# Gated SSM-convolution and shift-MLP kernel: the last transform step on two column tiles, its rows put in place by SBUF transfers, W4 in three tiles, and a new order of steps behind step 480

## The chip, the cores and the metric

The kernel runs on one core of a Trainium2 chip. The metric is the device time of one execution in microseconds (us). The engines are TensorE (PE; PEld is its weight load), VectorE (DVE), ScalarE (ACT), GpSimd (POOL) and SyncE (SP), which here issues nearly all DMAs.

## The reference, cut to what matters

```python
# q = B's x = A_q: 1 x 2048 x 640 (bf16); w1, w2: 640x640; w3: 640x1536; w4: 1536x640
def reference(A_q, A_k, A_v, A_shift_k, A_ssm_k, A_ssm_D, B_x, B_w1, B_w2, B_w3, B_w4, gate_w):
    x = A_q
    g = sigmoid((x * gate_w).sum(-1, keepdims=True))
    # a: a 4-tap shift of k, times v, a causal convolution over the 2048 rows, times q
    kv = shift4(A_k, A_shift_k) * A_v
    y = irfft(rfft(pad(kv), axis=1) * rfft(pad(A_ssm_k)).T)[:, :2048] + kv * A_ssm_D
    a = x * y
    # b: MLP with a row shift per quarter of the columns, then a second MLP
    h = gelu(layernorm(x) @ w1)
    x1 = x + shift_rows_by_quarter(h) @ w2
    b = x1 + gelu(layernorm(x1) @ w3) @ w4
    return g * a + (1 - g) * b
```

## The kernel before, in words

The 2048 rows lie as 128 partitions times 16 tiles `t1` (row = 16 p + t1), 640 columns each; four tiles are a chunk `c`. The result is built in place in the tile X (X1 is the same tile).

The convolution is a transform in four matmul steps with scratch in HBM between them. `step1` transforms the convolution's taps and kv along the partitions (scratch S_h, S_x). `gather` reads both back in blocks of 640 KB, `step2` transforms them along the tiles, `product` multiplies the two spectra on DVE, `step3` is the first half of the inverse and sends its blocks to the scratch S_g (8 sends, L523), and `gin` reads S_g back (L537) in three tiles: gin0 for t1 0 to 7, gin1 for t1 8 to 13, gin2 for t1 14 and 15, each by four loads `a` = 0 to 3. Load `a` needs the sends of the step3 calls 2a and 2a+1. gin1 lies in the place of W3, so its loads wait for the last matmul of `w3`.

`step4(t1)` is the last half of the inverse. A tile of 640 columns is done in two halves of 320. For each half the table F4 (128x128 bf16, two versions with zeros in every other column) is used in two matmuls, r = 0 and 1, that add up in one PSUM bank (L893). The row parity r thereby comes out interleaved on the partitions, as the rows of X lie. A half is then evicted in one of two ways: ACT copies it with the gate's factor as scale and DVE multiplies the copy with q (L897, L900), or DVE does both in one instruction on PSUM (L903). One DVE addition of 128x640 puts the tile onto X (L907).

The MLP runs beside it: `w3(c, f)` is five matmuls of 512 columns and a gelu on ACT (L840, L844), `w4(t1)` two halves of twelve matmuls of 320 columns and a DVE update of X (L867, L870; t1 = 14 is split into 512 and 128 columns and comes last). W4 is one tile of 1920 KB in the place of WA, which holds W1, W2 and a mixed part of W1; its one load (L216) therefore waits for the last matmul of `w2`.

The order of everything is a written list ORDER of 1099 names `call.arguments:step`. Each engine and SP executes its instructions in the order of this list and waits in place. SLOTS gives by hand which of 8 PSUM banks ("c") and which ring buffer each new tile takes. PE works in shapes: full 128x128 (`w3`, `w4`, `step4`), row tiles of 64 partitions (`step1`), 64x32 (`step2`) and 32x64 (`step3`).

## Time and profile before

| | before |
|---|---|
| times of three runs | 227.29, 228.85, 229.12 us (median 228.85) |
| profiled execution | 227.13 us, of which the span from first to last instruction is 225.4 us |
| PE, DVE, ACT busy | 217.8, 183.7, 171.4 us |
| PE share of the chain that ended last | 79% |
| bytes moved | 57.61 MB, mean 256 GB/s |
| granted TensorE clock | 1.000 |

A row of the chain of waits or of the timeline starts with its start and its length in us from the span's start. A row of the groups reads: line, engine, operation, out<-in, shapes, count | busy us, mean ns of one | idle us of that engine before it. A DMA row ends with KB of one transfer and the us from issue to landing.

### The profile page before, as it was taken

Reading aid. Unit: us, or ns where it says so; the run is one execution under the profiler, and the core shown is the slowest. Engines: PE = TensorE matmul, PEld = TensorE weight load, DVE = VectorE, ACT = ScalarE, POOL = GpSimd, SP = SyncE. Lnnn points to the kernel's source line nnn. Section 1 sums busy time; section 2 is a strip of 40 time slices with the busy share of each in tenths; the row PEclk is TensorE's granted clock in tenths of the full one; section 3 lists DMA queues with packets and bytes.
Section 4 is the critical chain, followed back from the end, with each engine's and each line's share of the span. In section 5 each row is a group of like instructions: output and inputs, shape, how many; then the busy total and the mean of one; then the engine's idle time right before and its main releaser. Section 6 shows DMA issues by size and latency. Waiting matters only on the chain.

```text
span 225.4 us, 6053 instructions
## 1 busy us (share of the span) xinstructions
PE 217.8 (97%) x2427; PEld 121.5 (54%) x2428; DVE 183.7 (81%) x447; ACT 171.4 (76%) x341; POOL 38.1 (17%) x91
## 2 busy tenths in 40 slices
PE   8989999899999999999999999999999999999994
PEld 2557455447846563345664444556533547657762
DVE  7898998868889969963899988989999841439994
ACT  4899988787999999999987597967988450266450
POOL 4247246816000431300600000000000000000000
PEclk9999999999999999999999999999999999999999
DMA  6999998892998999999989570690794879429914
GB/s 226 374 376 344 258 280 170 317 364 107 361 365 355 348 295 265 410 334 343 254 219 338 116 243 0 191 379 17 119 305 166 249 259 366 175 60 305 324 70 179
DMA packets 41770, 57.61 MB, mean 256 GB/s; under 512 B 18446, under 2 KB 34446, under 8 KB 41486
## 3 DMA queue, kind: packets, MB, share of 16 engines
q1 hardware_dynamic: 41166, 54.60, 75.4%
q0 software_dynamic: 576, 2.62, 3.1%
q8 instruction: 19, 0.31, 0.6%
q14 instruction: 9, 0.07, 0.1%
HBM read 34.93 MB, written 18.35 MB: 236 GB/s over the span
## 4 chain that ended last, share of the span: by engine, by line
PE 79%; DMA 9%; DVE 4%; ACT 4%; issue 1%; POOL 1%; SPq 0%; ACTq 0%
PE ps L840 24%; PE ps L867 23%; PE psw L788 7%; PE ps L465 5%; PE ps L893 4%; DMA X<-in_A_q_dram 4%; PE psm L707 4%; DMA xt<-xn 3%; PE psz L228 3%; PE ps L512 3%; PE ps L423 2%; PE pst L390 2%; DVE X L791 2%; ACT stg L360 2%; DMA S_x<-stg 2%; PE psk L590 1%
## 5 line engine op out<-in xcount | busy, mean ns | idle before, releaser
L840 PE MATMUL ps<-x1t,W 128*128 128x512 bf16 x240 | 56.1, 380 | 0.1
L867 PE MATMUL ps<-W,gt 128*128 128x320 bf16 (+2 forms) x383 | 55.1, 299 | 0.1
L867 PEld LDWEIGHTS <-gt 128*128 128x128 bf16 x384 | 36.2, 98 | 17.7 <-issue 3.0
L844 ACT ACTIVATE gt<-ps 128x512 bf16<-128x512 f32 x48 | 27.6, 609 | 19.0 <-PE ps L867 10.6
L840 PEld LDWEIGHTS <-W 128*128 128x128 bf16 x240 | 21.9, 98 | 28.7 <-issue 5.9
L360 ACT CAST stg<-ps 128x512 bf16<-128x512 f32 x55 | 28.6, 604 | 2.3 <-PE ps L423 2.0
L870 DVE SCALAR_TENSOR_TENSOR X<-ps,OMG,X 128x320 bf16<-128x320 f32 (+2 forms) x32 | 17.2, 547 | 11.9 <-PE ps L867 11.7
L707 PE MATMUL psm<-xt,WA 128*128 128x512 bf16 x100 | 23.4, 379 | 1.9 <-DMA WA<-in_B_w_dram 0.8
L360 ACT CAST gs<-ps 128x320 bf16<-128x320 f32 x41 | 15.6, 440 | 8.8 <-PE ps L512 4.8
L788 PE MATMUL psw<-WA,HT 128*128 128x320 bf16 x116 | 21.4, 300 | 0.0
L362 DVE CAST XS<-ps 128x512 bf16<-128x512 f32 x19 | 12.5, 684 | 6.7 <-PE ps L465 6.7
L362 DVE CAST stg<-ps 128x512 bf16<-128x512 f32 x25 | 15.8, 683 | 1.9 <-PE ps L423 1.9
L707 PEld LDWEIGHTS <-WA 128*128 128x128 bf16 x100 | 9.2, 97 | 12.9 <-DMA WA<-in_B_w_dram 1.0
L360 ACT CAST hs<-ps 128x512 bf16<-128x512 f32 x28 | 15.0, 605 | 1.4 <-PE ps L465 1.4
L791 DVE SCALAR_TENSOR_TENSOR X<-psw,X 128x320 bf16<-128x320 f32 x32 | 14.5, 487 | 1.6 <-PE psw L788 1.6
L897 ACT ACTIVATE y<-ps,GS 128x320 bf16<-128x320 f32 x22 | 10.4, 526 | 5.7 <-PE ps L893 3.5
L710 ACT ACTIVATE HT<-psm 128x512 bf16<-128x512 f32 x20 | 11.8, 617 | 3.6 <-PE psm L707 3.5
L788 PEld LDWEIGHTS <-HT 128*128 128x128 bf16 x116 | 10.7, 98 | 6.8 <-issue 3.1
L362 DVE CAST gs<-ps 128x320 bf16<-128x320 f32 x23 | 10.7, 484 | 2.4 <-PE ps L512 1.7
L797 ACT ACTIVATE jk<-X 128x640 bf16<-128x640 bf16 x16 | 12.2, 761 | 0.5 <-DVE X L791 0.4
L788 PE MATMUL psw<-WA,HM 128*128 128x320 bf16 x44 | 12.3, 299 | 0.0
L360 ACT CAST XS<-ps 128x512 bf16<-128x512 f32 x21 | 11.8, 607 | 0.5 <-PE ps L465 0.3
(151 smaller groups left out, 346.6 us busy)
## 6 DMA issues: line engine op xcount, KB each, us to landing
S_x<-stg SPq DMA_DIRECT2D x8, 640.0 KB, 4.3
S_h<-stg SPq DMA_DIRECT2D x8, 640.0 KB, 4.8
ax<-S_x SPq DMA_DIRECT2D x8, 640.0 KB, 5.9
ax<-S_h SPq DMA_DIRECT2D x8, 640.0 KB, 8.1
S_g<-gs SPq DMA_DIRECT2D x8, 640.0 KB, 3.6
W<-in_B_w_dram SPq DMA_DIRECT2D x2, 1920.0 KB, 9.1
kn<-in_A_k_dram SPq DMA_DIRECT2D x4, 640.0 KB, 6.9
E<-in_A_ssm_k_dram SPq DMA_DIRECT2D x5, 512.0 KB, 6.1
```

Of the source, the lines that this page charges most:

```text
L360: A.copy(out=dst, in_=src)
L362: V.tensor_copy(out=dst, in_=src)
L465: PE.matmul(ps[j][q:q + 32, lo - 512 * u:hi - 512 * u], lhsT=CMP[HALF[j], 8 * b + 4 * h + i, c, :], rhs=st[name, 2 * b + h][HALF[j], i, lo ...
L707: PE.matmul(ps[:].rearrange("p (a b) -> p a b", a=4), lhsT=W1N[:, k, 160 * u:160 * u + P] if u < 4 else W1M[:, k, :], rhs=xt[:, :, k, :], ...
L710: A.activation(out=st["HT"][:, 4 * c:4 * c + 4, u, :], in_=ps[:].rearrange("p (t b) -> p t b", t=4), func=ACT.Gelu_apprx_tanh)
L788: PE.matmul(ps[:], lhsT=h_tile(f, t1), rhs=W2P[:, f, o:o + W], start=(f == 0), stop=(f == 4))
L791: V.scalar_tensor_tensor(out=X1[:, t1, o:o + W], in0=box["ps"][:], scalar=1.0, in1=X[:, t1, o:o + W], op0=ALU.mult, op1=ALU.add, accum_out ...
L797: A.activation(out=jk[:], in_=X1[:, t1, :], func=ACT.Square, accum_out=S12[:, 1, t1:t1 + 1])
L840: PE.matmul(ps[:].rearrange("p (a b) -> p a b", a=4), lhsT=st["W3"][:, k, f * P:(f + 1) * P], rhs=xt[:, :, k, :], start=(k == 0), stop=(k ...
L844: A.activation(out=st["gt", c, f // 4][:, f % 4, :], in_=ps[:], func=ACT.Gelu_apprx_tanh)
L867: PE.matmul(ps[:], lhsT=st["gt", c, f // 4][:, f % 4, i * P:(i + 1) * P], rhs=st["W4"][:, f, o:o + w], start=(f == 0), stop=(f == FC - 1))
L870: V.scalar_tensor_tensor(out=X1[:, t1, o:o + w], in0=box["ps"][:], scalar=OMG[:, t1:t1 + 1], in1=X1[:, t1, o:o + w], op0=ALU.mult, op1=ALU ...
```

## The change

Up to step 480 of ORDER (about 89 us into the span) the two kernels do the same work in the same order. The change has three parts.

1. `step4` now takes a chunk of four tiles. For each half of 320 columns the two parities r are two matmuls of 128x64 weights into the two partition halves of one bank, on two column tiles. The eviction (ACT or DVE) scales by GSP, the gate's factor in the order of parities, into a tile `ys`. When the eight halves of a chunk are evicted, two DMAs of 64 partitions and 320 KB each (L907 of the changed kernel) put the even and the odd rows in place in a tile YP. Then DVE multiplies with q in two instructions of 128x1280 and adds to X in two more.
2. WA is three tiles, and W4 comes in three loads of 800, 800 and 320 KB into them.
3. ORDER has 1074 names, in a new order behind step 480.

```diff
-    F4 = const.tile([P, 2, H, 2], BF16, name="F4")
+    F4 = const.tile([P, H], BF16, name="F4")
+    GSP = const.tile([P, NT], F32, name="GSP")
...
-    WA = main.tile([P, DC * (2 * D + P)], BF16, name="WA", tag="WA")
...
+    WN = main.tile([P, DC, D], BF16, name="WN", tag="WN")
+    WP = main.tile([P, DC, D], BF16, name="WP", tag="WP")
+    WM = main.tile([P, DC, P], BF16, name="WM", tag="WM")
+    W1N, W2P, W1M = WN[:], WP[:], WM[:]
...
-    def load_w4():
-        st["W4"] = main.tile([P, FC, D], BF16, name="W4", tag="WA")
-        SP.dma_start(out=st["W4"][:], in_=B_w4.rearrange("(kt p) e -> p kt e", p=P))
+    def load_w4(u):
+        n, w = ((0, DC), (DC, DC), (2 * DC, 2))[u]
+        st["W4", u] = main.tile([P, w, D], BF16, name="W4" + "abc"[u], tag=("WN", "WP", "WM")[u])
+        SP.dma_start(out=st["W4", u][:], in_=B_w4.rearrange("(kt p) e -> p kt e", p=P)[:, n:n + w, :])
...
-        V.memset(F4[:], 0.0)
-        yield from sin_table(F4[:, 0, :, 0], n, 256)
-        A.activation(out=F4[:, 1, :, 1], in_=n[:], func=ACT.Sin, scale=TWO_PI / 256 * SH, bias=NPI[:])
+        yield from sin_table(F4[:], n, 256)
...
+        yield
+        for r in range(2):
+            SP.dma_start(out=GSP[HALF[r], :], in_=GS[r:P:2, :])
...
-    def step4(t1, ev):
...
-                    PE.matmul(ps[:], lhsT=F4[:, r].rearrange("p a b -> p (a b)"), rhs=g[:, r, o + 320 * v:o + 320 * v + 320], start=(r == 0), stop=(r == 1))
...
+    def step4(c, ev):
+        box = {}
+        def make(u):
+            t1, w = 4 * c + u // 2, slice(320 * (u % 2), 320 * (u % 2) + 320)
+            part = [z for z in range(3) if GIN[z][0] <= t1][-1]
+            o = (t1 - GIN[part][0]) * D + 320 * (u % 2)
+            ps = []
+            def first():
+                ps.append(slot(psc, [P, 320], F32, "ps5", "c", 8))
                 for r in range(2):
+                    PE.matmul(ps[0][HALF[r], :], lhsT=F4[:], rhs=st["gin", part][:, r, o:o + 320], start=True, stop=True, tile_position=(0, H * r))
+            def second():
+                if "ys" not in box:
+                    box["ys"] = slot(pool("L2"), [P, 4, D], BF16, "hs", "hp", 4)
+                scaled(ev[u], box["ys"][:, u // 2, w], ps[0][:], GSP[:, t1:t1 + 1])
+            return [first, second]
+        def send():
+            if "YP" not in st:
+                st["YP"] = main.tile([P, 4, 4, D], BF16, name="YP", tag="RT")
+            for r in range(2):
+                SP.dma_start(out=flat(st["YP"][r:P:2, c]), in_=flat(box["ys"][HALF[r]]))
+        def times(h):
+            y = st["YP"][:, c, 2 * h:2 * h + 2, :]
+            V.tensor_tensor(out=y, in0=y, in1=st["q2", c][:, 2 * h:2 * h + 2, :], op=ALU.mult)
+        def total(h):
+            x = X1[:, 4 * c + 2 * h:4 * c + 2 * h + 2, :]
+            V.tensor_tensor(out=x, in0=x, in1=st["YP"][:, c, 2 * h:2 * h + 2, :], op=ALU.add)
+        return banks(8, make, [send, lambda: times(0), lambda: times(1), lambda: total(0), lambda: total(1)])
...
-        "step1.HT0.0.VAAVVAVAVV:12 "
-        "w3.0.6:1 "
...
+        "step1.HT0.1.VVAAAAAAVA:16 load_w4.1:0 w3.0.8:0 w3.0.8:1 w3.0.6:1 step1.HT0.0.VAAVVVVAAV:7 w2.15:4 w3.0.4:0 "
...
```

The following pieces show the order of instructions at the three places that the prediction speaks of. S_h, S_x and S_g are the scratches, stg and gs what is sent to them, ax and gin what is read back, ys appears under the name hs, q2 is q.

SP's queue around the load of W4, before (from about 90 us into the span):

```order
L437 DMA S_h_69<-stg_1726 128x2560
L437 DMA S_h_69<-stg_1812 128x2560
L437 DMA S_h_69<-stg_1844 128x2560
L216 DMA W4_2090<-in_B_w4_dram 128x12x640
L444 DMA ax_2138<-S_h_69 128x4x640
```

and in the changed kernel:

```order
L218 DMA W4b_1845<-in_B_w4_dram 128x5x640
L437 DMA S_h_69<-stg_1727 128x2560
L218 DMA W4c_1980<-in_B_w4_dram 128x2x640
L437 DMA S_h_69<-stg_1813 128x2560
L437 DMA S_h_69<-stg_1842 128x2560
L218 DMA W4a_2155<-in_B_w4_dram 128x5x640
L444 DMA ax_2189<-S_h_69 128x4x640
```

Two of the three parts of W4 now stand ahead of the last sends to S_h, which the first read of S_h waits for.

SP's queue from the last sends to S_g to the end, before:

```order
L523 DMA S_g_71<-gs_3601 128x4x640
L876 DMA q2_3757<-in_A_q_dram 128x2560
L537 DMA gin0_3437<-S_g_71 32x2x5120 x2
L537 DMA gin2_3568<-S_g_71 32x2x1280
L876 DMA q2_3819<-in_A_q_dram 128x2560
L537 DMA gin1_3832<-S_g_71 32x2x3840 x4
L876 DMA q2_3989<-in_A_q_dram 128x2560
L855 DMA out_0_dram<-X_102 128x1280 x6
```

and in the changed kernel:

```order
L523 DMA S_g_71<-gs_3569 128x4x640
L537 DMA gin0_3310<-S_g_71 32x2x5120
L537 DMA gin2_3314<-S_g_71 32x2x1280
L907 DMA YP_3783<-hs_3691 64x2560 x2
L879 DMA q2_3803<-in_A_q_dram 128x2560
L879 DMA q2_3805<-in_A_q_dram 128x2560
L537 DMA gin2_3314<-S_g_71 32x2x1280
L858 DMA out_0_dram<-X_103 128x1280
L537 DMA gin2_3314<-S_g_71 32x2x1280
L879 DMA q2_3850<-in_A_q_dram 128x2560
L537 DMA gin1_3868<-S_g_71 32x2x3840 x4
L907 DMA YP_3783<-hs_3838 64x2560 x2
```

The first transfer to YP, a store and two loads of q now stand between the last load of gin0 and the loads of gin1. On PE, sixty matmuls of `w4` and five of `w3` stand between the last `step3` and the first `step4` of the changed kernel.

DVE's last rows, before (the end of the queue, 12 rows):

```order
L900 TENSOR_TENSOR q2_3989<-y_4018,q2_3989 128x320
L900 TENSOR_TENSOR q2_3819<-y_4023,q2_3819 128x320
L870 SCALAR_TENSOR_TENSOR X_102<-ps4_4027,OMG_98,X_102 128x320
L907 TENSOR_TENSOR X_102<-X_102,q2_3819 128x640
L900 TENSOR_TENSOR q2_3819<-y_4060,q2_3819 128x320
L907 TENSOR_TENSOR X_102<-X_102,q2_3819 128x640
L900 TENSOR_TENSOR q2_3989<-y_4064,q2_3989 128x320
L870 SCALAR_TENSOR_TENSOR X_102<-ps4_4045,OMG_98,X_102 128x320
L900 TENSOR_TENSOR q2_3989<-y_4042,q2_3989 128x320
L907 TENSOR_TENSOR X_102<-X_102,q2_3989 128x640 x3
L870 SCALAR_TENSOR_TENSOR X_102<-ps4_4067,OMG_98,X_102 128x512
L870 SCALAR_TENSOR_TENSOR X_102<-ps4_4091,OMG_98,X_102 128x128
```

and in the changed kernel, from the last eviction of `step4` on DVE:

```order
L349 TENSOR_SCALAR hs_3940<-ps5_3967,GSP_80 128x320
L911 TENSOR_TENSOR YP_3783<-YP_3783,q2_3850 128x1280 x2
L915 TENSOR_TENSOR X_103<-X_103,YP_3783 128x1280 x2
L873 SCALAR_TENSOR_TENSOR X_103<-ps4_3986,OMG_99,X_103 128x320
L873 SCALAR_TENSOR_TENSOR X_103<-ps4_4000,OMG_99,X_103 128x320
L911 TENSOR_TENSOR YP_3783<-YP_3783,q2_3805 128x1280 x2
L915 TENSOR_TENSOR X_103<-X_103,YP_3783 128x1280 x2
L911 TENSOR_TENSOR YP_3783<-YP_3783,q2_3454 128x1280 x2
L915 TENSOR_TENSOR X_103<-X_103,YP_3783 128x1280 x2
L873 SCALAR_TENSOR_TENSOR X_103<-ps4_4039,OMG_99,X_103 128x320
L873 SCALAR_TENSOR_TENSOR X_103<-ps4_4059,OMG_99,X_103 128x512
L873 SCALAR_TENSOR_TENSOR X_103<-ps4_4017,OMG_99,X_103 128x128
```

All multiplications and additions of three of the four chunks now stand in one block behind the last eviction; before they were spread between the evictions tile by tile.

## Prediction

> **What bounds the kernel now.** I read the page first (busy time and slices), then the shares of the chain, then busy time by stage, then the end of the chain.

> ```profile
> PE 217.8 (97%) x2427; PEld 121.5 (54%) x2428; DVE 183.7 (81%) x447; ACT 171.4 (76%) x341; POOL 38.1 (17%) x91
> PE   8989999899999999999999999999999999999994
> DVE  7898998868889969963899988989999841439994
> PE 79%; DMA 9%; DVE 4%; ACT 4%; issue 1%; POOL 1%; SPq 0%; ACTq 0%
> ```

> ```profile
> 89.00:120.00 31.00, 31.00 (x402) 16.02 (x402) 23.36 (x44) 29.74 (x62) 5.90 (x18) 1.00 1.01 315
> 120.00:150.00 30.00, 30.00 (x359) 14.83 (x358) 27.58 (x46) 23.49 (x48) 0.00 (x0) 1.00 0.62 190
> 150.00:183.00 33.00, 32.99 (x432) 15.93 (x430) 30.53 (x48) 23.51 (x55) 0.00 (x0) 1.00 0.67 200
> 183.00:200.00 17.00, 17.00 (x107) 10.34 (x106) 4.25 (x10) 4.85 (x9) 0.00 (x0) 1.00 0.56 208
> 200.00:225.40 25.40, 21.94 (x161) 15.14 (x159) 20.59 (x56) 11.88 (x25) 0.00 (x0) 1.00 0.61 207
> ```

> ```profile
> 200.25 5.16 PE ps L893 x38
> ...
> 219.00 2.34 PE ps L867 x10
> ...
> 221.36 1.02 DVE X L870 x2
> ```

> In the stage rows the first figure is the length of the stretch, then busy time of PE, PEld, DVE, ACT and POOL, the clock, the DMA share and GB/s. From 89 us on, exactly where the order is new, PE is busy in every microsecond until 221.33. The chain there is PE alone. So PE time that is taken away counts in full, but there is no slack on PE either: each new wait of PE costs its full length. Behind PE's last matmul stand 1.05 us of DVE (to 222.38) and 3.0 us of store (to 225.4).

> **PE work taken away.** All 64 matmuls of `step4` are on the chain: 38 in 5.16 us is 0.136 each, so 8.7 us. After, they are 32 pairs on two column tiles. Whether a pair runs at once this trace shows only for four column tiles of 32 (L719), and what a change of shape costs it shows in `w4`:

> ```profile
> 46.63 1.05 PE L719 MATMUL psz<-xt,GWR 128*32 128x512 bf16 x16
> 122.09 2.27 PE ps L840 x10
> 105.01 5.00 PE ps L867 x36
> 110.78 1.74 PE ps L867 x12
> 205.95 1.29 DVE L907 TENSOR_TENSOR X<-X,q 128x640 bf16<-128x640 bf16 x3
> L907 DVE TENSOR_TENSOR X<-X,q 128x640 bf16<-128x640 bf16 x16 | 7.4, 484 | 0.0
> L486 DVE TENSOR_TENSOR p<-XS,hs 128x1280 bf16<-128x1280 bf16 x8 | 6.5, 816 | 0.5 <-ACT hs L360 0.5
> 203.55 1.78 ACT L897 ACTIVATE y<-ps,GS 128x320 bf16<-128x320 f32 x4 [0.41 <-PE ps L893]
> L870 DVE SCALAR_TENSOR_TENSOR X<-ps,OMG,X 128x320 bf16<-128x320 f32 x30 | 16.2, 547 | 11.6 <-PE ps L867 11.3 <-ACT hs L360 0.2
> L870 DVE SCALAR_TENSOR_TENSOR X<-ps,OMG,X 128x512 bf16<-128x512 f32 x1 | 0.8, 751 | 0.4 <-PE ps L867 0.4
> out_dram<-X SPq DMA_DIRECT2D x7, 320.0 KB, 3.2
> out_dram<-X SPq DMA_DIRECT2D x1, 128.0 KB, 1.7
> ```

> One after another, 16 matmuls of 512 columns would take 16 x 0.136 x 512/320 = 3.5 us; L719 took 1.05. So I take full overlap: 32 x 0.136 = 4.35 us, a gain of **4.35** (ends: 0 if pairs don't overlap, 4.35).

> A run of 12 `w4` matmuls behind another shape takes 1.74, while 24 more add 5.00 - 1.74, 1.63 for each 12: a change of shape costs 0.11. Behind step 480 the old order has 64 runs of one shape, the new one 69 (three of them column tiles): **+0.55** (0 to 0.8).

> **The tail.** Let R be the start of the last run of 13 column pairs. Until the end PE has those (1.8, with shape changes 2.0) and four halves of `w4` and w4(14): 3 x 1.63 + 3.26 = 8.15; PE ends at R+10.1. DVE's last rows begin with its eviction of the ninth pair, which ends about R+1.9 (nine pairs 1.2, shape 0.1, eviction about 0.5). An instruction of 128x1280 is shown with 816 ns, and back to back the 640 form comes 0.08 closer (three in 1.29 against 484 ns each), so I take 0.74; four make 3.0. First chunk: R+4.9. Two `w4` updates of 0.47 (547 ns, less 0.08), the second held by its matmuls: R+5.9. The second chunk waits for its transfer: ACT's sixth eviction ends at R+2.9 (four in 1.78), two issues of 0.35, landing 3.2 as a store of the same 320 KB: R+6.5, done R+9.5. The third chunk has landed by then (its send stands behind a store that needs R+4.9; R+8.8), done R+12.5. Three updates, of 320, 512 and 128 columns, 0.47, 0.67 and some 0.3: R+13.9. DVE thus ends 3.8 behind PE, against 1.05 before: **+2.75**. The SBUF transfer has no row; its ends are the 1.7 us of the 128 KB store (the wait of 0.6 goes) and the 5.4 of a 640 KB read (below), which is 2.2 more. I take 3.2, the row of equal size. The GSP loads (two, of 64 partitions) and the work on F4 that goes lie tens of us ahead of their use: nothing.

> **New waits for DMAs.** With PE full, only landing times can open gaps. Three places are tight.

> ```profile
> 181.33 0.41 PE ps L512 x16
> 182.66 0.88 DVE L362 CAST gs<-ps 128x320 bf16<-128x320 f32 x2
> 183.90 0.37 SPq L523 DMA_DIRECT2D S_g<-gs  x1
> 187.45 0.52 SPq L537 DMA_DIRECT2D gin<-S_g  x1
> gin<-S_g SPq DMA_DIRECT2D x1, 640.0 KB, 5.4
> gin<-S_g SPq DMA_DIRECT2D x4, 160.0 KB, 3.9
> 200.28 2.46 SPq L537 DMA_DIRECT2D gin<-S_g  x4
> gin<-S_g SPq DMA_DIRECT2D x4, 480.0 KB, 4.0
> ```

> (a) The last `step3` to gin0. Before, PE finishes it at 181.74, the send goes at 183.90, the read at 187.45 (3.55 later, when the send has landed) and lands 5.4 later at 192.9: 11.1 us, and PE first uses gin0 at 200.25. In the new order DVE has four evictions behind it (two in 0.88, so 1.75, send at +2.0): 2.0 + 3.55 + 5.4 = 11.0 us. PE has five halves of `w4` and one `w3` group in between: 5 x 1.63 + 1.08 + 0.11 = 9.3. PE waits **1.7** (ends: 0.2 if the read lands in 3.9, like the small ones; 4.4 if it takes the 8.1 of the reads of S_h in (b); 5.4 is the same read in the same place).

> (b) W4 and S_h.

> ```profile
> 94.77 0.38 SPq L216 DMA_DIRECT2D W<-in_B_w_dram  x1
> W<-in_B_w_dram SPq DMA_DIRECT2D x1, 1920.0 KB, 9.6
> 105.08 0.91 SPq L444 DMA_DIRECT2D ax<-S_h  x2
> ax<-S_h SPq DMA_DIRECT2D x2, 640.0 KB, 6.8
> ax<-S_h SPq DMA_DIRECT2D x8, 640.0 KB, 8.1
> 109.94 0.85 PE L465 MATMUL ps<-ax,CMP 64*32 64x128 bf16 x40
> ```

> From 89 to 120 the DMA share is 1.01, so the order of transfers only moves who is late. The new order puts 1120 KB of W4 ahead of the last sends to S_h; the sum of bytes until W4 is complete stays, so it lands at about 104.4 as before, where PE wants it at about 104.5. PE then reaches `step2` of h one half of `w4` earlier (109.94 - 1.63 - 0.4 of shape changes, 107.9), and the third read of S_h at 110.8, which landed at 105.08 + 6.8 = 111.9. I take **+0.7** (0 to 2). (c) gin2's last load now waits behind a store that waits for DVE; it would be issued 3.5 us ahead of its use, against 3.9 for such a load: **+0.2** (0 to 1). gin1: four loads in 2.46 and 4.0 for the last, 6.5, against 6.6 of PE work: nothing, with no margin.

> **Sum.** -4.35 + 0.55 + 2.75 = -1.05 without new waits; +1.7 + 0.7 + 0.2 gives +1.55. The profiled span goes from 225.4 to 227.0, its execution from 227.13 to 228.7. The runs shown have a median of 228.85, 1.7 above that execution; added there, **230.4 us**, +0.7%.

> **Rivals.** *Landings at their slow ends* (slower): if the transfers to YP land like the 640 KB read, 5.4 instead of 3.2, the second chunk in the tail starts 2.2 later and everything behind it too, and PE's place is not on the path any more: 230.4 + 2.2 = 232.6, slower. It decides from a landing of 3.9 on, where +0.7 more is used up. For it: each is two transfers in a queue that also carries stores. Against: half the bytes, and no HBM on either side.

> *PE's gain is undone by banks* (slower): 32 evictions at 0.42 on two engines take 6.7 us, more than the 4.35 of their matmuls, and the last run puts 13 pairs into 8 banks, with ten evictions on ACT, 4.2 us. If PE goes at the pace of evictions in all three runs, it ends 2.4 later, 232.8. Against: `w4` halves of 1.63 between and behind the runs need one bank each, and the run needs only five banks freed early, which costs some 0.3 that the lagging DVE hides. [...]

> *The column pairs don't overlap*: +4.35 on PE, of which the part behind R is hidden by DVE (13 x 0.136 = 1.8): 230.4 + 2.6 = 233.0. L719 speaks against it.

> *The tail is covered* (faster): DVE keeps up, as it does before, and no landing is late: 228.85 - 4.35 + 0.55 = 225.05. Against it stand twelve instructions of 0.74 behind the last run, 8.9 us of DVE that nothing in the new queue lets start earlier.

> **Chances.** About 1% (2.3 us) is what a measurement of this kernel can tell from no change; within it lie 226.6 to 231.1. My forecast, within 1%: 0.52. Slow landings 0.27, banks 0.08, no overlap 0.06: slower by more than 1% 0.41. Covered tail: faster 0.07. The range: without new waits 227.8 (228.85 - 1.05), which is the low end; the high end holds the three slow rivals, 232.6 to 233.0, so 233.0. The likeliest case's own range is 227.8 to 231.1.

> **What would show it.** Right: no PE idle inside the three runs of column pairs, and 22 matmuls of the second run in 1.5 us; an idle of PE of 1 to 3 us ahead of the first `step4` put down to DMA gin; DVE busy nearly without gaps from the last run to the end, 3 to 4 us beyond PE's last matmul; PE waits of about 1 us on ax between 107 and 113. Wrong: PE full until the end (then the time is 229 or less), a gap in DVE's last block of over 2 us ahead of a multiplication into YP (slow landings), or gaps of PE in 120 to 180 us, where I looked for late landings and found none.

## The result and the profile after

The changed kernel takes 235.37 us (median of 234.65, 235.13, 235.61 and 237.52), the kernel before beside it 228.71 (227.29 to 229.12): ratio 1.032, 95% interval 1.024 to 1.040. It is slower by 3.2%, and outside the range of the prediction. The profiled execution takes 234.65 us, its span is 232.9 us, 7.5 more than before.

The page's busy time, and the shares of the chain that ended last:

```profile
PE 213.0 (91%) x2428; PEld 117.9 (51%) x2428; DVE 184.8 (79%) x427; ACT 168.3 (72%) x337; POOL 38.6 (17%) x91
PE 64%; DMA 19%; DVE 10%; issue 2%; SPq 2%; POOL 1%; DVEq 0%; ACT 0%
```

PE has 4.8 us less to do than before, but its share of the chain falls from 79 to 64%, and DMA's rises from 9 to 19%. The work that was taken away was replaced by waits for transfers. The list of waits (engine, what it ran, what it waited for: us in total, times, longest) names them:

```profile
PE ps L895 <- DMA gin<-S_g: 3.2, 3, 1.1
DVE YP L911 <- DMA YP<-hs: 2.6, 2, 1.8
PE ps L465 <- DMA ax<-S_h: 1.0, 1, 1.0
```

The timeline of PE shows where; the bracket at a row's end is the idle time ahead of it.

```profile
189.63 1.28 PE L895 MATMUL ps<-gin,F 128*64 128x320 bf16 x16 [0.98 <-DMA gin<-S_g]
...
204.47 0.33 PE L895 MATMUL ps<-gin,F 128*64 128x320 bf16 x2
...
205.93 1.55 PE L895 MATMUL ps<-gin,F 128*64 128x320 bf16 x20 [1.14 <-DMA gin<-S_g]
...
212.41 0.33 PE L895 MATMUL ps<-gin,F 128*64 128x320 bf16 x2
...
213.78 2.03 PE L895 MATMUL ps<-gin,F 128*64 128x320 bf16 x24 [1.04 <-DMA gin<-S_g]
...
223.52 0.59 PE L870 MATMUL ps<-W4c,gt 128*128 128x512 bf16 x2
```

Each of the three runs of column pairs waits about 1 us for gin, the first ahead of it, the second and the third behind their first pair. Otherwise PE doesn't stop inside a run, so the pairs do overlap, at 0.16 us a pair (16 matmuls, 8 pairs, in 1.28). PE ends at 224.11. DVE ends 6.0 us later, and the chain shows why:

```profile
206.42 7.23 DMA gin<-S_g
215.68 1.56 DVE YP L911 x2
217.24 1.47 DVE X L915 x2
219.97 5.41 DMA YP<-hs
225.47 1.56 DVE YP L911 x2
```

```profile
228.60 1.47 DVE L873 SCALAR_TENSOR_TENSOR X<-ps,OMG,X 128x320 bf16<-128x320 f32 x3
```

gin1's last load took 7.23 us, the last transfer into YP 5.41. The end follows two landings and DVE's work behind them.

### The profile page after: what moved, and what is told of

It reads as the page before. It is cut to its first block, busy times and chain, and to the rows that moved or that the text cites. A ratio compares the mean times of both kernels' runs of the same rounds, so it can differ in the third digit from the quotient of the medians.

```text
span 232.9 us, 6040 instructions
## 1 busy us (share of the span) xinstructions
PE 213.0 (91%) x2428; PEld 117.9 (51%) x2428; DVE 184.8 (79%) x427; ACT 168.3 (72%) x337; POOL 38.6 (17%) x91
## 4 chain that ended last, share of the span: by engine, by line
PE 64%; DMA 19%; DVE 10%; issue 2%; SPq 2%; POOL 1%; DVEq 0%; ACT 0%
PE ps L843 22%; PE ps L870 12%; PE psw L788 7%; PE psm L707 6%; DMA gin<-S_g 5%; DMA WN<-in_B_w_dram 4%; PE ps L465 4%; PE ps L423 3%; DMA ax<-S_h 3%; DMA xt<-xn 3%; PE ps L512 3%; PE pst L390 2%; DMA YP<-hs 2%; DVE X L791 2%; DMA S_g<-gs 2%
## 5 line engine op out<-in xcount | busy, mean ns | idle before, releaser
L870 PEld LDWEIGHTS <-gt 128*128 128x128 bf16 x384 | 36.0, 98 | 17.6 <-issue 3.2
L360 ACT CAST stg<-ps 128x512 bf16<-128x512 f32 x55 | 28.5, 605 | 2.3 <-PE ps L423 2.1
L873 DVE SCALAR_TENSOR_TENSOR X<-ps,OMG,X 128x320 bf16<-128x320 f32 (+2 forms) x32 | 16.9, 545 | 13.6 <-PE ps L870 13.3
L870 PE MATMUL ps<-W4a,gt 128*128 128x320 bf16 (+2 forms) x160 | 27.1, 300 | 0.1
L870 PE MATMUL ps<-W4b,gt 128*128 128x320 bf16 (+2 forms) x160 | 27.0, 300 | 0.0
L707 PE MATMUL psm<-xt,WN 128*128 128x512 bf16 x80 | 18.8, 380 | 2.9 <-DVE xt L362 1.5
L788 PE MATMUL psw<-WP,HT 128*128 128x320 bf16 x116 | 21.4, 300 | 0.0
L360 ACT CAST gs<-ps 128x320 bf16<-128x320 f32 x42 | 15.9, 435 | 7.3 <-PE ps L512 6.4
L362 DVE CAST stg<-ps 128x512 bf16<-128x512 f32 x25 | 16.0, 684 | 3.2 <-PE ps L423 3.2
L360 ACT CAST hs<-ps 128x512 bf16<-128x512 f32 x32 | 16.8, 614 | 2.1 <-PE ps L465 1.8
L347 ACT ACTIVATE hs<-ps,GSP 128x320 bf16<-128x320 f32 x21 | 9.2, 539 | 6.9 <-PE ps L895 6.9
L362 DVE CAST XS<-ps 128x512 bf16<-128x512 f32 x20 | 13.1, 682 | 1.1 <-PE ps L465 1.0
L870 PE MATMUL ps<-W4c,gt 128*128 128x320 bf16 (+2 forms) x64 | 13.9, 299 | 0.0
L362 DVE CAST gs<-ps 128x320 bf16<-128x320 f32 x22 | 10.0, 485 | 4.2 <-PE ps L512 4.1
L707 PEld LDWEIGHTS <-WN 128*128 128x128 bf16 x80 | 7.3, 98 | 11.7 <-DVE xt L362 1.7
L465 PE MATMUL ps<-ax,CMP 64*32 64x128 bf16 (+3 forms) x512 | 12.0, 299 | 1.0 <-DMA ax<-S_h 1.0
```

What stands on the lines that cost most here:

```text
L347: A.activation(out=dst, in_=src, func=ACT.Copy, scale=a)
L360: A.copy(out=dst, in_=src)
L362: V.tensor_copy(out=dst, in_=src)
L465: PE.matmul(ps[j][q:q + 32, lo - 512 * u:hi - 512 * u], lhsT=CMP[HALF[j], 8 * b + 4 * h + i, c, :], rhs=st[name, 2 * b + h][HALF[j], i, lo ...
L707: PE.matmul(ps[:].rearrange("p (a b) -> p a b", a=4), lhsT=W1N[:, k, 160 * u:160 * u + P] if u < 4 else W1M[:, k, :], rhs=xt[:, :, k, :], ...
L788: PE.matmul(ps[:], lhsT=h_tile(f, t1), rhs=W2P[:, f, o:o + W], start=(f == 0), stop=(f == 4))
```

## The experiments

Ratios are to the kernel before, run on the same chip beside each experiment. All start from the changed kernel, except the first, which starts from the kernel before. Lines of ORDER stand for moves.

### Column tiles alone, in the old order

```diff
-                    PE.matmul(ps[:], lhsT=F4[:, r].rearrange("p a b -> p (a b)"), rhs=g[:, r, o + 320 * v:o + 320 * v + 320], start=(r == 0), stop=(r == 1))
+                    PE.matmul(ps[HALF[r], :], lhsT=F4[:], rhs=g[:, r, o + 320 * v:o + 320 * v + 320], start=True, stop=True, tile_position=(0, H * r))
```

> The kernel before in its own order and with its one W4 load; only the two matmuls of each half in the last step are two column tiles. The rows are not put in place (the two parities stay in the two halves of the partitions). Theory 'the pairs overlap and PE's gain is real, but the last 22 us of before are nearly as full on DVE as on PE': PE saves 4.35 us, DVE (20.6 us busy from 200 to 225) lets 1 to 2.5 of it through: 226.2 to 227.7 us against 228.7. Rival 'pairs do not overlap': 228.7. Rival 'PE's gain counts in full': 224.4.

Measured: 228.75 us against 228.44, ratio 0.9997 (0.9947 to 1.0047). None of the 4.35 us shows in the time; the interval leaves room for 1.2. The first run of pairs on PE:

```profile
203.13 1.57 PE L891 MATMUL ps<-gin,F 128*64 128x320 bf16 x16
204.86 1.57 PE L891 MATMUL ps<-gin,F 128*64 128x320 bf16 x14 [0.17 <-ACT gt L842]
206.75 0.46 PE L891 MATMUL ps<-gin,F 128*64 128x320 bf16 x4 [0.31 <-DVE q L901]
207.44 0.46 PE L891 MATMUL ps<-gin,F 128*64 128x320 bf16 x4 [0.23 <-DVE q L901]
```

38 matmuls take 4.8 us from first to last, against 5.3 before in the same view: after eight pairs PE starts to wait for ACT and DVE, 0.17, 0.31 and 0.23 us. From the first run to its last matmul PE needs 20.8 us for 21.9 before, so some 1.1 us arrive on PE; a wait of 1.1 for ACT at 107.89 takes them back in this profile. In this order the waits, 0.71 us in a run of 19 pairs, speak for the prediction's rival of the banks; at 0.16 a pair the run would take 3.0, and the rest of the difference has no wait beside it. In the new order, with runs of 8, 11 and 13, the pairs of the changed kernel take 5.5 us in all (1.28 + 0.33 + 1.55 + 0.33 + 2.03), against 8.7 before: some 3.2 of the 4.35 arrive.

### No transfers into YP

```diff
         def send():
-            if "YP" not in st:
-                st["YP"] = main.tile([P, 4, 4, D], BF16, name="YP", tag="RT")
-            for r in range(2):
-                SP.dma_start(out=flat(st["YP"][r:P:2, c]), in_=flat(box["ys"][HALF[r]]))
+            pass
 
-            y = st["YP"][:, c, 2 * h:2 * h + 2, :]
+            y = box["ys"][:, 2 * h:2 * h + 2, :]
```

> The changed kernel without its eight SBUF transfers: DVE multiplies the evicted halves where they lie, so the rows are not put in place. Theory 'slow landings of the transfers (5.3 us each) and their issues on SP hold the tail': the 2.6 us that DVE waits for YP go, and the reads of gin1 land earlier: 3 to 4 us less, 231.5 to 232.5 against 235.4. Rival 'the block of twelve long DVE instructions holds the tail, the transfers are hidden': 235 or more.

Measured: 236.17 us, ratio 1.034 (1.028 to 1.039): no gain. That is the number of the rival, but not for its reason. The chain and PE's timeline at the first run of pairs:

```profile
180.39 6.69 DMA S_g<-gs
187.16 4.28 DMA gin<-S_g
```

```profile
191.47 2.34 PE L895 MATMUL ps<-gin,F 128*64 128x320 bf16 x16 [3.56 <-DMA gin<-S_g]
193.75 4.13 PE L843 MATMUL ps<-x1t,W 128*128 128x512 bf16 x10
```

```profile
190.00:195.00 5.00, 3.52 (x19) 1.68 (x20) 2.31 (x5) 1.40 (x4) 0.00 (x0) 0.56 0.94 383
```

Up to here the two kernels have the same order, yet the last send to S_g landed after 6.69 us, against 4.25 in the changed kernel's profile, and PE stood 3.56 us. Behind the gap the granted clock (the third column from the end of the stretch's row) is 0.56, and the same matmuls take longer: 2.34 against 1.28, and 4.13 against 2.33 for ten of `w3`. A gap of 3.6 us thus cost 3.6 and 2.9 more. The tail did get shorter, as expected: DVE ends 13.5 us behind the start of the last 24 matmuls, against 16.3. The gap hid it. All four executions seem to have it: their mean granted clocks are 0.979 to 0.980, while those of the changed kernel are 0.992, 0.991, 0.989 and 0.983.

### W4's loads late

```diff
-load_w4.1 ... load_w4.2 ... step1 (last sends to S_h) load_w4.0
+step1 (last sends to S_h) load_w4.1 load_w4.2 load_w4.0
```

> The changed kernel with the first two W4 loads moved behind the last sends to S_h, directly ahead of the third. Theory 'two thirds of W4 ahead of the sends delay the first reads of S_h': PE's wait of 1.0 us ahead of step2 of h goes, 234.4 against 235.4. Rival 'the DMA queue is full there and only changes who is late': 235.4, PE then waits for W4 or for the third read of S_h.

Measured: 238.47 us, ratio 1.041 (1.036 to 1.046), worse than the changed kernel. PE's first half of `w4`:

```profile
108.48 1.16 PE L870 MATMUL ps<-W4a,gt 128*128 128x320 bf16 x5 [2.38 <-DMA W4a<-in_B_w_dram]
109.44 1.54 PE L870 MATMUL ps<-W4b,gt 128*128 128x320 bf16 x5
```

The wait moved from S_h (1.0) to W4 (2.4), and behind it five matmuls take 1.16 and 1.54 in place of 0.84. The order of W4's loads is therefore not where the time was lost; sending two of them early is the better side.

### SP's order of late loads

```diff
-step4.0:16 load_q.0 load_q.2 gin.2.1 store.1 gin.2.2 load_q.1 gin.1.0 gin.1.3 gin.1.2 gin.1.1
+step4.0:16 gin.2.1 gin.2.2 load_q.0 load_q.2 store.1 gin.1.0 gin.1.3 gin.1.2 gin.1.1 load_q.1
...
-store.2 ... step4.3:16
+step4.3:16 store.2
```

> The changed kernel with only SP's order changed: the last two gin2 loads ahead of the q loads and the first store, the third q load behind the gin1 loads, the send of the last chunk to YP ahead of the store that waits for DVE. Theory 'waits in SP's queue make the landings late': PE's wait of 1.1 us for gin2 goes, that of 1.0 for gin1 shrinks, the last chunk of the tail starts 0.8 earlier: 232.5 to 233.5 against 235.4. Rival 'the landings are slow by themselves, not by their place in the queue': within 0.5 us of 235.4.

Measured: 237.6 us, ratio 1.038 (1.031 to 1.045).

```profile
191.73 2.34 PE L895 MATMUL ps<-gin,F 128*64 128x320 bf16 x16 [3.73 <-DMA gin<-S_g]
...
209.51 1.76 PE L895 MATMUL ps<-gin,F 128*64 128x320 bf16 x22
...
218.51 2.03 PE L895 MATMUL ps<-gin,F 128*64 128x320 bf16 x24 [1.99 <-DMA gin<-S_g]
```

gin2's wait is gone: 22 matmuls in one piece. But gin0 has the long gap again, with matmuls at 2.34, and gin1 waits 2 us. One wait was cured, two others grew. Up to gin0 the order is that of the changed kernel, so the long gap is not shown to come from this edit, and the time doesn't judge it.

### No wait for gin, with and without transfers

```diff
-rhs=st["gin", part][:, r, o:o + 320]
+rhs=INV[:].rearrange("p a b c -> p (a b c)")[:, 320 * r:320 * r + 320]
```

> The changed kernel, with the 64 matmuls of step4 reading a constant table (INV) in place of gin0, gin1 and gin2; every load, send and store stays in its place in the queues. So step4 works on other data. Theory A (late landings of gin hold PE): the three waits of 0.98, 1.14 and 1.04 us go, 3.2 us; no idle of PE from 120 us to its last matmul, and the granted clock stays at 1.00 there. 235.4 - 3.2 = 232.2 us, or less if some executions of the changed kernel have a gin0 gap of 3.6 us with a low clock behind it, as the runs without transfers and with the other SP order had. Theory B (DVE and the transfers into YP set the end whatever PE does): PE is done earlier, DVE is not, 235 us.

Measured: 232.3 us, ratio 1.016 (1.004 to 1.027): 3.1 less than the changed kernel, near the 3.2 of theory A, though the intervals of the two ratios overlap a little. In its profile no idle time of PE is left behind 120 us, but DVE now waits longer for YP, 4.8 us in place of 2.6:

```profile
DVE YP L911 <- DMA YP<-hs: 4.8, 2, 3.0
```

The second run has the change to `send` and `times` from above as well:

> The run above, and no transfers into YP either: DVE multiplies the evicted tile as it stands, so rows are not put in place. Theory A (landings alone make the loss, and they add): 232.2 less 2.7 (without transfers DVE ended 13.7 us behind the start of the last run of pairs, with them 16.5), 229.5 us; within 1% of the kernel before. Theory B (DVE's own work in the tail is the bound): no better than 232. A clock that drops although nothing waits would speak against the gaps as its cause.

Measured: 226.57 us, ratio 0.989 (0.979 to 0.999). The last run of pairs and DVE's last row:

```profile
209.54 2.17 PE L895 MATMUL ps<-INV,F 128*64 128x320 bf16 x26
```

```profile
221.70 1.47 DVE L873 SCALAR_TENSOR_TENSOR X<-ps,OMG,X 128x320 bf16<-128x320 f32 x3
```

DVE ends 13.6 us behind the start of the last run. So the tail's 13.9 of the prediction was right but for its transfer. Taking the waits for gin away is worth 3.1 us, taking the transfers into YP away 5.7 more, twice the 2.7 of theory A; that fits the 4.8 us for which DVE waited for YP in the run before. Without both, the kernel would be 1.1% faster than before (0.1 to 2.1%), so the whole loss lies in these landings and the sends that go with them.

### Sends in halves

```diff
-            for r in range(2):
-                SP.dma_start(out=flat(st["YP"][r:P:2, c]), in_=flat(box["ys"][HALF[r]]))
+            for h in range(2):
+                for r in range(2):
+                    SP.dma_start(out=flat(st["YP"][r:P:2, c, 2 * h:2 * h + 2]), in_=flat(box["ys"][HALF[r], 2 * h:2 * h + 2]))
```

> The changed kernel, with each send into YP cut in two by columns: first the two halves of 64 partitions for the first 1280 columns, then those for the second, four transfers of 160 KB in place of two of 320 KB. Theory A (landing goes by bytes: two of 320 KB are 640 KB, and 640 KB take 5.3 us as elsewhere in this trace): the first half lands 3 to 4 us behind its issue, and DVE's wait ahead of the last two multiplications shrinks by 1 to 2 us: 233.5 to 234.5 us. Theory B (a fixed price of a transfer between partitions): landing stays above 5 us, the two more issues of 0.4 come on top: 235.4 to 236.5 us.

Measured: 235.55 us, ratio 1.033 (1.021 to 1.044). From the chain, and PE's timeline:

```profile
219.40 3.91 DMA YP<-hs
```

```profile
214.61 3.41 PE L895 MATMUL ps<-gin,F 128*64 128x320 bf16 x24 [3.14 <-DMA out_dram<-X]
```

A part of 160 KB can land sooner than one of 320 (3.91 against 5.41), so there is no fixed price of 5 us. But the chunk as a whole, from its first send (217.61) to DVE's multiplication (223.33), takes 5.7 us, against 5.2 (216.37 to 221.59) in the changed kernel: its 640 KB landed no sooner in four parts than in two. DVE's waits for YP fall from 2.6 to 0.2 us, in part because it waits 1.5 for late matmuls of `w4` instead. The last run of pairs waited 3.14 us and then ran at 3.41 in place of 2.03. The row puts that wait down to a store, which these matmuls don't read; what they need is gin1, whose last load was issued at 205.92 and took 8.6 us.

### More work ahead of gin0

```diff
-step4.0 (eight pairs) ... w4.9:2 w4.8:0 ... w4.9:3 ... w4.8:1
+w4.9:2 w4.9:3 w4.8:0 w4.8:1 step4.0 (eight pairs)
```

> The changed kernel with two halves of w4 (w4(9) second half, w4(8) first half, their matmuls and updates) moved from behind the first run of step4 to ahead of it: 3.3 us more of PE work between the last step3 and gin0's first use. The PSUM banks behind that place are given out anew. Theory A (gaps of PE at gin0 cost their length, and a drop of the clock where they are 2 us or longer): no idle of PE at gin0, clock 1.00 in 185 to 205 us; 235.4 - 1.0 = 234.4 us, and the spread of times gets smaller. Theory B (gin1's landing sets the end, so the wait only moves there): 235.4 us with a longer wait ahead of the last run of pairs.

Measured: 236.8 us, ratio 1.031 (1.018 to 1.044), no gain. No idle time at gin0 any more, but this on the timeline of DVE, SP and PE:

```profile
200.95 1.56 DVE L911 TENSOR_TENSOR YP<-YP,q 128x1280 bf16<-128x1280 bf16 x2 [4.96 <-DMA q<-in_A_q_dram]
...
203.40 0.34 SPq L858 DMA_DIRECT2D out_dram<-X  x1
203.79 0.57 SPq L537 DMA_DIRECT2D gin<-S_g  x1
...
206.64 2.88 PE L895 MATMUL ps<-gin,F 128*64 128x320 bf16 x20 [4.50 <-DMA gin<-S_g]
```

Read from top to bottom, this is one chain: a late q holds DVE, DVE holds the store, the store holds gin2's last load in SP's queue, and PE stands 4.5 us, after which 20 matmuls take 2.88 in place of 1.55. Neither theory named this place. The 2 us of theory A for a drop of the clock were the author's estimate: behind a gap of 2.16 us in the run without transfers 24 matmuls took 2.03, as at full clock.

### The gap filled

This starts from the run without transfers.

```diff
                 ps.append(slot(psc, [P, 320], F32, "ps5", "c", 8))
+                if c == 0 and u == 3:
+                    for _ in range(14):
+                        PE.matmul(ps[0][:], lhsT=IDB[:], rhs=INV[:].rearrange("p a b c -> p (a b c)")[:, 0:320], start=True, stop=True)
                 for r in range(2):
```

> The run without transfers into YP (rows not put in place; 236.2 us, gap of 3.56 at gin0, clock 0.56 behind it) with 14 matmuls of 128x320 on constant tables put on PE right ahead of the first column pair: 1.9 us of work that needs no load and whose result is overwritten. Theory A (an idle PE of 3 to 4 us makes the clock drop): the idle time at gin0 shrinks to 1.7 us, the clock stays at 1.00 in 190 to 200 us, and the 16 pairs' matmuls take 1.28 again, not 2.34: 236.2 - 2.9 = 233.3 us although PE does more. Theory B (the drop comes from something else, such as the load of DMA or the time since the start): the clock is still below 0.8 there, 236 us or more.

Measured: 232.14 us, ratio 1.012 (1.005 to 1.020), 4 us less than without the filling. PE's timeline of one execution (the longest of the four, 234.35):

```profile
186.41 2.07 PE L896 MATMUL ps<-INV,IDB 128*128 128x320 bf16 x14
190.41 1.28 PE L898 MATMUL ps<-gin,F 128*64 128x320 bf16 x16 [1.93 <-DMA gin<-S_g]
...
214.95 3.39 PE L898 MATMUL ps<-gin,F 128*64 128x320 bf16 x24 [2.69 <-DMA gin<-S_g]
```

The landing is as late as before (S_g's send took 7.15), but with 1.93 us idle in place of 3.56 the pairs take 1.28 again. In the same execution the unfilled gap of 2.69 at gin1 is followed by slow matmuls. Work that computes nothing made this version faster.

### All late loads mended

gin1 moves to the space of RT, so that it doesn't wait for `w3`'s end, and the loads go ahead; sends in halves and more work ahead of gin0 stay.

```diff
-main.tile([P, 2 * n * D], BF16, name="gin1", tag="W3") if q == 1
+rt()[:, 0:2 * n * D] if q == 1
...
-gin.0.2 gin.2.3 step4.0:16 load_q.0 load_q.2 gin.2.1 store.1 gin.2.2 load_q.1 gin.1.0 gin.1.3 gin.1.2 gin.1.1
+gin.0.2 gin.2.3 gin.2.1 gin.2.2 load_q.0 gin.1.0 gin.1.3 gin.1.1 gin.1.2 step4.0:16 load_q.2 store.1 load_q.1
```

> The changed kernel, whole computation, with its late loads mended: gin1 lies in the space of RT (free since 167 us) in place of W3's and is loaded right behind gin0; gin2's last two loads and the first q load ahead of it; YP's first chunk behind gin1 in RT, the others in W3's space; each send into YP cut in two as in the run of split sends; the third store behind the last send; two halves of w4 ahead of the first run of step4 as in the run with more work ahead. Theory A (the loss is late landings, which is all that this takes away): no idle of PE above 1 us from 120 us on, clock 1.00; 226.6 us of the run without gin and without transfers, and 1 to 2 us for the last chunk's transfer: 228 us (227 to 229.5). Theory B (DMA has no room, whatever the order): 2.5 MB more ahead of 200 us push gin0 or q back, and a gap of PE comes back there: 232 us or more.

Measured: 230.25 us, ratio 1.007 (1.003 to 1.011). No gap of PE in its profile behind 120 us is above 0.5 us, the clock stays at 1.00, and 5 us of the loss are back; a little less than theory A expected. The last part of YP's first chunk, behind gin1's 1920 KB, took 7.0 us. PE's longest wait and that landing:

```profile
203.43 0.92 PE L900 MATMUL ps<-gin,F 128*64 128x320 bf16 x6 [0.50 <-DVE hs L349]
```

```profile
194.09 7.04 DMA G1Y<-hs
```

Two further steps:

```diff
-load_q.0 gin.1.0 gin.1.3 gin.1.1 gin.1.2 step4.0:16
+load_q.0 step4.0:16 gin.1.0 gin.1.3 gin.1.1 gin.1.2
...
-w4.13:2 w4.13:3 ... step4.3 (last pairs) w4.15:2 w4.15:3
+step4.3 (last pairs) w4.13:2 w4.15:2 w4.13:3 w4.15:3
```

> The run with gin1 early (230.25 us, DVE ends 4.6 behind PE), with two moves: YP's first sends go ahead of gin1's four loads, and one half of w4(13) goes from ahead of the last run of column pairs to behind it, so that run starts 1.63 us sooner. Whole computation. Theory A (with the loads early, only DVE's block behind the last run sets the end): end 1 to 1.6 us sooner, DVE's wait for YP's first chunk of 3.7 gone, 228.7 to 229.3 us, level with the kernel before. Theory B (ACT's and DVE's evictions of the second run hold the banks, so the last run can't start sooner): 230 us, with PE idle for PSUM ahead of the last run.

Measured: 227.53 us against 228.12, ratio 1.000 (0.997 to 1.004). And with `w4.13:0` and `w4.13:1` behind the last run as well:

> The run above with the other half of w4(13) behind the last run of pairs as well, so only one half of w4 stands between the second and the third run. Theory A: the last run starts up to 3.3 us sooner than in the run with gin1 early, DVE ends with PE: 227 to 228.5 us. Theory B: ACT needs 0.43 us for each of 17 evictions, 7.3 us for both runs, so PE waits 1 to 2 us for banks inside the third run, and no more than in the run above is won: 229 to 230 us.

Measured: 227.82 us against 228.12, ratio 0.998 (0.995 to 1.002). The last run and DVE's end, of the first of the two and then of the second:

```profile
207.93 2.37 PE L900 MATMUL ps<-G1Y,F 128*64 128x320 bf16 x24
...
222.17 1.47 DVE L878 SCALAR_TENSOR_TENSOR X<-ps,OMG,X 128x320 bf16<-128x320 f32 x3
```

```profile
207.34 2.37 PE L900 MATMUL ps<-G1Y,F 128*64 128x320 bf16 x24
...
220.77 0.59 PE L875 MATMUL ps<-W4c,gt 128*128 128x512 bf16 x2
...
223.05 1.47 DVE L878 SCALAR_TENSOR_TENSOR X<-ps,OMG,X 128x320 bf16<-128x320 f32 x3
```

Both do the whole computation and are level with the kernel before, 3% faster than the changed one. So column pairs, transfers into YP and W4 in three tiles don't have to cost 3%; the places of loads, sends and tiles and of some halves of `w4` decide. What each of these moves is worth alone was not measured. No version that does the whole computation is faster than before beyond its interval. The second move starts the last run 0.6 us sooner, not 1.6, in an execution in which PE also had a wait of 1.5 for S_h.

## Why the prediction was wrong, point by point

The two profiled executions, term by term, in us. The last line before the sum, PE's start behind step 480, is the shift of the row that was 88.91 before and is 90.07 now, for the same work ahead:

```profile
88.91 1.24 PE L840 MATMUL ps<-x1t,W 128*128 128x512 bf16 x5
```

```profile
90.07 2.10 PE L843 MATMUL ps<-x1t,W 128*128 128x512 bf16 x9
```

| term | predicted | measured |
|---|---|---|
| column pairs | -4.35 | about -3.2 (5.5 for 8.7) |
| changes of shape | +0.55 | not measured apart |
| S_h, W4 | +0.7 | +1.0 |
| gin0 | +1.7 | +0.98 |
| gin2 | +0.2 | +1.14 |
| gin1 | 0 | +1.04 |
| DVE behind PE | +2.75 | +5.6 (6.0 for 0.4) |
| start | 0 | +1.15 |
| sum | +1.55 | +7.7 without shapes; the spans differ by 7.5 |

One reading of the prediction is off here: it let PE end at 221.33, where the chain passes to DVE, but PE's last row before ends at 221.99. DVE ended 0.4 us behind it and not 1.05, so the prediction's own 3.8 for after makes +3.4, not +2.75.

```profile
215.31 6.68 PE L867 MATMUL ps<-W,gt 128*128 128x320 bf16 x47
```

The start differs between executions (88.2 to 90.7 in the profiles of the experiments, which have the same work ahead of it), so it belongs to the execution. The medians are 6.7 apart. The 1.7 us that the prediction added, from the profiled execution to the median, were 0.7 here.

**The step that failed first**, and by the most, is the transfer into YP, "I take 3.2, the row of equal size". Two transfers of 320 KB go together, and what lands is 640 KB: 5.2 to 5.5 us, the figure of the rival of slow landings. In the run with sends in halves the same 640 KB took 5.7. The rival priced the tail well: it put DVE's end 16.1 behind the last run of pairs (13.9 and 2.2), and it came 16.3 behind the row of 213.78. But it looked for one wait, of over 2 us; there were two, since the third chunk, which the prediction let land in time, was late too:

```profile
221.59 1.56 DVE L911 TENSOR_TENSOR YP<-YP,q 128x1280 bf16<-128x1280 bf16 x2 [1.77 <-DMA YP<-hs]
...
225.47 1.56 DVE L911 TENSOR_TENSOR YP<-YP,q 128x1280 bf16<-128x1280 bf16 x2 [0.84 <-DMA YP<-hs]
```

**The second** is gin1, "nothing, with no margin", and gin2 at 0.2. gin1's landing was taken from the kernel before, where nothing else was in the queue. Here a store of 320 KB, gin2's 160, q's 640, gin1's 1920 and YP's 640 KB are issued between 202.8 and 210.7, and the last load of gin1 took 7.2 in place of 4.0. YP's sends are not what made it late: without them it took 7.09. That it is the other bytes is argued, not shown by a run of its own. gin2's load stood behind a store that waited for DVE, as the prediction said, but DVE in turn waited for q:

```profile
200.34 1.56 DVE L911 TENSOR_TENSOR YP<-YP,q 128x1280 bf16<-128x1280 bf16 x2 [1.69 <-DMA q<-in_A_q_dram]
```

**The third** is that pairs cost 0.16 to 0.17 and not 0.136: some +1.1 in all.

**gin0** was priced within its bounds, 0.98 in the profile for 1.7, but its wait differs between executions of the same order, from 0.8 to 3.7, because S_g's last send lands after 4.0 to 7.2 us. What decides this was not found: the mean DMA share of 180 to 185 us was 0.72 in the changed kernel and 0.90 in the run without transfers, no more is shown.

**What no term covered** is the price of a gap beyond its length. In the changed kernel's own profile, gaps of about 1 us left the clock at 1.00. Its longest execution (237.52) may hold a longer gap: its mean clock is 0.983, against 0.992 in the profiled one. There is no trace of it.

**What was right**: PE never idles between 120 and 180 us; the pairs overlap; PE waits for S_h between 100 and 120; DVE's work in the tail, without its transfer, is 13.6 (predicted 13.3, as 13.9 held 0.6 of wait); and the sum without new waits, -1.05, fits the run without late landings (0.979 to 0.999 of before, so -4.8 to -0.2). So it was mostly the landings' sizes that were off, and they added up because each stood on the path.

## What to carry to other kernels

Price a transfer by all bytes that stand in the queue with it, not by a row of the same size from a quiet place, and count two halves of one send as one (here 5.2 to 5.5 us where the row said 3.2, and 7.2 for gin1's last load where it said 4.0). When the bounding engine has no slack, move each load ahead of every store that waits for another engine before taking work away from it (behind such a store, a load of gin2 held PE for 4.50 us in one run); the same change cost 3% or nothing, by where its loads, its sends and some of PE's work stood. Mending one place alone won nothing in five runs here, because another landing was late in its turn; to see the whole price, take all such waits away at once in one run.

## What the runs showed of the hardware

| idle time of PE, us | run | matmuls behind it, us (the same at full clock) |
|---|---|---|
| 0.98, 1.14, 1.04 | changed kernel | 16 in 1.28, 20 in 1.55, 24 in 2.03 |
| 1.93 | gap filled | 16 in 1.28 |
| 1.99 | SP's order | 24 in 2.03 |
| 2.16 | no transfers | 24 in 2.03 |
| 2.38 | W4 late | 5 in 1.16, 5 in 1.54 (0.84 each) |
| 2.69 | gap filled | 24 in 3.39 (2.03) |
| 3.14 | sends in halves | 24 in 3.41 (2.03) |
| 3.56 | no transfers | 16 in 2.34 (1.28) |
| 3.73 | SP's order | 16 in 2.34 (1.28) |
| 4.50 | more work ahead | 20 in 2.88 (1.55) |

Filling one such gap with matmuls until 1.93 us of 3.56 were left kept the speed. Whether the length of the idle time alone decides is not shown.

The two rows below are from the run with sends in halves; in each the length comes first, then PE's busy time, and the clock is third from the end. The gap of 3.14 us is spread over both: PE idles for 1.95 us of the first and 1.19 of the second.

```profile
210.01:213.42 3.41, 1.46 (x11) 0.75 (x9) 0.72 (x2) 0.53 (x1) 0.00 (x0) 1.00 0.98 321
213.42:220.25 6.83, 5.64 (x33) 3.65 (x34) 4.34 (x7) 4.17 (x9) 0.00 (x0) 0.50 0.37 105
```

So a gap's price is more than its length. In the second row PE was busy for 5.64 us at a clock of 0.50; an estimate from these two numbers is that half of the time, 2.8 us, came on top of the gap. In the run without transfers it was 2.9, by the times of the matmuls behind the gap of 3.56.
